# Wider score passes, joined weights and moved means in the first two units of a fused attention and MoE kernel

## The chip, the cores and the metric

The kernel runs on one core of one Trainium2 chip. A core has a matmul engine (TensorE, PE in the profile, with its weight loads as PEld), a vector engine (VectorE, DVE), an activation engine (ScalarE, ACT), a general one (GpSimd, POOL) and a queue that issues the transfers (SyncE, SP). The metric is the device time of one execution in microseconds; lower is better.

## The reference

Attention with a local window plus block summaries, then one expert layer (MoE) on its result. The weights are handed to the kernel as 8-byte floating-point words, and the kernel turns them into 4-byte ones itself.

```python
B, H, S, D = 4, 8, 768, 64          # batch elements, heads, positions, head size
k_sum = k.reshape(B, H, 24, 32, D).max(axis=3)      # 24 block maxima
v_sum = v.reshape(B, H, 24, 32, D).mean(axis=3)     # 24 block means
scores_l = q @ k.T / 8, masked to |i - j| < 16      # local window
scores_s = q @ k_sum.T / 8 + log(32)
a = softmax(concat(scores_l, scores_s))
x = (a @ concat(v, v_sum))           # 3072 tokens x 512
h = x @ w_in                         # 512 x 2048
out = (h - tanh(h)) @ w_out          # 2048 x 512
```

## The kernel before, in words

The work is cut into eight units of 384 rows, two to a batch element, so units 0 and 1 are the first element. A unit's attention goes over four pairs of heads (two pairs make a group), and a pair over three tiles of 128 rows. Per tile: one score product for both heads; `softmax`, whose step "min" adds the mask and takes the smallest (negated) score, then "exp", "sum guard", "inverse" and "normal"; `transpose_probs` ("p turn" on TensorE, "p out" back to SBUF); `values`. A row of scores has SC = 182 columns, but each half of a tile (64 rows) needs only N2 = 118 of them, shifted by 64 between the halves: `softmax` therefore runs "min" once for each half, and everything after on 118 columns.

The MoE of a unit goes over 16 slices f of the hidden dimension: `moe_in`, `moe_act`, `moe_split`, `moe_out`. In unit 0 the weights are used whole, in plain float32; each weight is then split into a high and a low part (`split_whole`) for the later units, which use three faster products instead of one. `convert` makes a float32 weight from the 8-byte words: "w scale" scales the high words, "w shift" shifts the result by three bits, "w low" joins the three bits from the low words, and "w sign" joins the sign. These three run on VectorE, one behind the other, for each of 32 weights.

Block means: for the first element `first_means` loads all values of a group and sums them with six products ("sum"). For the other three elements `sum_chunks` loads chunks and adds them on VectorE ("chunk sum"), and `finish_v` turns the sums with TensorE. `put_mean` writes the means into the values buffer `vw` by a transfer. `rawq` (queries) and `vw` (values) are one buffer each, used by the two groups in turn.

The order is made by a planner. The loop at the end of `program` adds tasks with their costs and dependences; `Plan.schedule` simulates the engines with these costs and a priority (the length of the way to the end, moved by the tables `BIAS` and `KB`), picks an engine where a task has several (`either`, tempered by `SL`), and the instructions are issued in the order found. Each engine then runs its own list in order. While TensorE has nothing to do in the first 100 us of that plan, "keep warm" products are put in. The MoE of unit 0 is added 22 slots behind its attention, so it runs beside the attention of unit 1. Tiles of one tag share a ring of buffers: a new tile waits until the oldest is released. All instructions of the program have one line in the profile, L64, that of a helper; tiles tell them apart: `prob` and `stat` are the softmax, `pS`, `pY`, `pT`, `pX`, `pH` banks of PSUM, `raw` the loaded weight words, `tmp` and `qa` their work buffers, `wf` whole weights, `wh` high parts, `chunk` and `vacc` the chunk sums, `xh` with `blk` the first sums.

The program is followed by a second version of itself under a condition that these inputs do not meet.

Of the kernel before, what the change touches and what calls it, by code (L numbers as in the profile page):

```python
# [12 lines left out]
U32 = mybir.dt.uint32  # L13
I32 = mybir.dt.int32
# [19 lines left out]
BIAS = {('top turn', 6): -62, ('p out', 19): -34, ('series', 46): -24, ('sum guard', 39): 21, ('p turn', 21): 39, ('q turn', 8): 13, ('square', 3): 43, ('w load', 29): 33, ('exp', 139): 10, ('x high', 7): 25, ('square', 16): -7, ('exp', 47): 33, ('series', 95): -20, ('square', 15): 11, ('w load', 17): 10, ('w sign 2', 2): 20, ('values', 23): -12, ('w scale', 7): 30, ('top turn', 4): 19, ('w load', 25): -40, ('square', 13): 19, ('inverse', 21): 44, ('p turn', 19): -20, ('w sign', 2): 26, ('out', 13): -36, ('min', 142): 21, ('series', 11): 10, ('normal', 25): -15, ('p out', 23): 32, ('pick', 8): 55, ('normal', 47): -11, ('v load', 13): 43, ('mean out', 3): 7, ('direct', 11): -29, ('w load', 15): -31, ('v load', 44): 24, ('out', 14): -34, ('exp', 44): -17, ('square', 8): 4, ('w load', 27): 16, ('min', 39): 60, ('g', 9): -24, ('inverse', 19): 36, ('direct', 14): 20, ('w high part', 23): -4, ('q high', 8): 12, ('w high part', 21): -20, ('cube', 1): 21, ('normal', 44): -4, ('in', 8): 8, ('w sign', 10): -32, ('in', 1): 24, ('normal', 24): -17, ('sum', 1): -20, ('x low', 7): -31, ('k load', 35): -9, ('square', 11): 1, ('tanh', 6): 20, ('v load', 39): -20, ('square', 9): 8, ('normal', 46): -8, ('direct', 6): 1, ('k high', 25): -5, ('q low', 6): 60, ('q high', 2): 30, ('inverse', 67): -5, ('w shift', 29): -5, ('v load', 52): 30, ('min', 5): -5, ('p turn', 8): -60, ('top put', 12): 60, ('min', 74): -30, ('chunk load', 5): -5, ('values', 17): 5, ('exp', 102): -60, ('values', 26): -30, ('square', 33): 30, ('w high part 2', 9): 5, ('inverse', 45): 15, ('normal', 83): -15, ('top put', 3): 30, ('k again', 9): 60, ('w low part 2', 0): -5, ('square', 73): -60, ('q again', 39): -60, ('values', 15): 5, ('k turn', 13): -5, ('sum guard', 15): -15, ('q again', 6): -60, ('exp', 24): -15, ('in', 28): -60, ('scores', 70): -15, ('w low part 2', 24): -60, ('scores', 43): 5, ('exp', 11): 5, ('normal', 36): -30, ('w shift', 19): 30, ('series', 24): 60, ('k high', 3): 15, ('q load', 15): -5, ('p out', 74): -15, ('out', 6): -30, ('min', 56): 30, ('w low part 2', 15): -5, ('out', 80): -30, ('scores', 23): -60, ('out', 41): -60, ('p turn', 87): 5, ('sum guard', 29): -30, ('chunk load', 23): -30, ('out', 3): 60, ('min', 60): -15, ('series', 20): 60, ('values', 9): 15, ('w high part 2', 16): -30, ('sum guard', 52): 30, ('normal', 8): -60, ('min', 33): 5, ('q again', 29): 60, ('exp', 18): 15, ('g low', 2): -30, ('q turn', 0): -15, ('k turn', 12): -30, ('values', 1): -60, ('series', 0): 30, ('k again', 6): -15, ('const', 2): 15, ('out', 295): 15, ('out', 85): 60, ('out', 2): -5, ('out', 45): 60, ('scores', 16): -30, ('v load', 51): -5, ('const', 10): -15, ('series', 99): -30, ('k high', 22): -15, ('min', 34): 15, ('w high part 2', 21): 30, ('k high', 55): -15, ('q load', 7): -5, ('inverse', 13): -5, ('k high', 27): -15, ('top put', 23): -60, ('w low', 21): 5, ('p out', 38): -60, ('out', 76): -30, ('out', 307): 15, ('x low', 2): -30, ('in', 126): -30, ('q load', 9): -30, ('out', 75): -5, ('w low', 13): -60, ('p out', 26): 30, ('exp', 75): 15, ('sum guard', 50): 60, ('w shift', 11): 5, ('values', 6): 30, ('chunk sum', 3): -30, ('inverse', 3): 30, ('sum guard', 42): -15, ('tanh', 1): 60, ('top max', 11): -15, ('w shift', 14): 15, ('v load', 27): 15, ('v load', 79): -5, ('series', 19): -15, ('sum guard', 90): 15, ('in', 66): -60, ('q again', 23): 30, ('p out', 18): 5, ('in', 35): -5, ('pad', 0): 5, ('w scale', 19): -5, ('g', 19): -5, ('in', 40): 30, ('p out', 25): -30, ('k high', 12): -30, ('v load', 60): -30, ('k load', 12): -60, ('sum guard', 74): -60, ('scores', 17): 30, ('k high', 7): -15, ('sum guard', 21): 60, ('p turn', 27): 30, ('q low', 42): 30, ('out', 87): 15, ('w high part 2', 22): 60, ('top put', 38): -15, ('w low', 2): 30, ('w high part 2', 26): -5, ('top put', 69): 15, ('top put', 39): -30, ('w scale', 2): -30, ('tanh', 15): -35, ('w high part 2', 17): -30, ('v load', 3): 15, ('p turn', 81): 15, ('min', 164): 5, ('p out', 6): 5, ('exp', 48): -60, ('exp', 176): -60, ('tanh', 77): -15, ('q again', 14): 30, ('exp', 22): -30, ('p out', 12): -30, ('exp', 43): -5, ('min', 2): 5, ('k turn', 15): 30, ('sum guard', 16): 60, ('v load', 37): 15, ('square', 23): -5, ('top put', 13): -5, ('tanh', 31): -60, ('v load', 81): 15, ('tanh', 37): -30, ('x low', 6): -30, ('tanh', 57): 15, ('w low part 2', 14): 30, ('p turn', 93): -15}  # L34
# [3 lines left out]
SL = {('sum guard', 0, 'gpsimd'): 0.6, ('top put', 1, 'vector'): 0.6, ('cube', 2, 'vector'): -0.3, ('g low', 2, 'vector'): 0.3, ('q high', 1, 'vector'): 0, ('x high', 1, 'vector'): -0.3, ('w scale', 0, 'vector'): 0.6, ('cube', 1, 'vector'): -0.3, ('big', 1, 'scalar'): -0.3, ('w low part 2', 1, 'vector'): 0.6, ('q again', 1, 'scalar'): 0.6, ('q again', 2, 'scalar'): 0, ('top put', 2, 'vector'): 0, ('w high part 2', 1, 'vector'): -0.3, ('sum guard', 1, 'gpsimd'): -0.6, ('top low', 1, 'gpsimd'): -0.3, ('k again', 1, 'gpsimd'): -0.6, ('sum guard', 2, 'gpsimd'): 0, ('q high', 0, 'vector'): 4, ('x whole', 2, 'vector'): 1.5, ('normal', 2, 'scalar'): 0, ('x high', 2, 'vector'): -0.6, ('w scale', 1, 'vector'): 2.5, ('top put', 0, 'scalar'): 0.6, ('k high', 2, 'vector'): 0.6, ('p out', 2, 'vector'): 1, ('p out', 1, 'vector'): 2.5, ('w high part 2', 2, 'vector'): 0, ('top put', 0, 'vector'): 2.5, ('k again', 1, 'scalar'): 1.5, ('k high', 1, 'vector'): 1, ('top high', 1, 'scalar'): -0.6, ('top high', 2, 'scalar'): 0.3, ('g', 1, 'vector'): 0.6, ('p out', 0, 'vector'): 1.5, ('q again', 2, 'gpsimd'): 0, ('x high', 0, 'vector'): 0.3, ('q high', 2, 'vector'): 0.3}  # L38
# [17 lines left out]
class Engine:  # L56


    def __init__(self, tc, engine):
        self._tc, self._engine = tc, engine  # L60

    def __getattr__(self, name):
        op = getattr(self._engine, name)
        return lambda *args, **kwargs: self._tc.keep_in_program_order(op(*args, **kwargs))  # L64


class Task:
    __slots__ = ("index", "costs", "go", "after", "order", "level", "count", "ready", "next", "start", "engine", "cost", "place", "out", "banks", "behind", "moves", "kind", "name")

HELD = {"w shift", "w low", "w sign", "w low part", "w low part 2", "w low part 3", "w high part", "w high part 2", "w scale", "normal", "g high", "g low", "g", "cube", "big", "k again", "q again", "top pre", "sum guard"}
# [23 lines left out]

class Plan:

    SEEN = {PE: 0.2, ACT: 0.16, DVE: 0.13, POOL: 0.1, SP: 0.95}
    ISSUE = 0.5
    QUEUE = 3.0
    AHEAD = 1.1

    def __init__(self):  # L110
# [47 lines left out]
    def schedule(self, idle):  # L158
# [49 lines left out]
        while total:  # L208
            best = None
            for e in engines:  # L210
                if able[e]:
                    now = max(free[e], min(ready(t, e) for t in able[e]))
                    if e == SP:
                        now = max(now, dma - self.QUEUE)
# [864 lines left out]
```

## Time and profile before

| | us |
|---|---|
| median of 3 runs | 762.74 |
| lowest, highest | 762.58, 763.68 |
| the profiled execution | 762.32 |
| its span, first to last instruction | 760.6 |
| TensorE busy | 718.8 (95%) |
| VectorE busy | 497.6 (65%) |
| ScalarE busy | 481.0 (63%) |
| GpSimd busy | 202.2 (27%) |

Busy times are sums over one execution. The digits of a slice are tenths of its length. Rows of a group give the tile written and those read, shapes, the count, busy time in us and mean duration in ns, and then the idle time of the engine just before, with what ended it. Rows of a timeline give start and length in us.

### The profile page before, as it was taken

The page shows a single profiled execution, that of the slowest core. Times are in us where ns is not written, and L with a number is a line of the kernel's source. Part 1 is how long each engine was busy: PE and PEld are TensorE (multiplying, and loading weights), DVE is VectorE, ACT ScalarE, POOL GpSimd, SP SyncE. Part 2 cuts the span into 40 slices and gives each one's busy share as a digit, 9 for nine tenths or more (in the row PEclk, how much of TensorE's full clock was granted, in tenths as well). Part 3 has the DMA queues.
Part 4 walks back from the last instruction along what each step waited for, and adds up shares of the span by engine and source line. Part 5 has one row for each costly group of instructions (what it writes and reads, how often), then busy time and mean ns, then how long its engine had stood idle before and what let it go on. Part 6 is the DMA issues. An engine that isn't in the chain of part 4 may idle for free. (4 is left out here: it accounts for less than half of the span.)

```text
span 760.6 us, 13191 instructions
## 1 busy us (share of the span) xinstructions
PE 718.8 (95%) x4187; PEld 584.8 (77%) x4187; DVE 497.6 (65%) x1789; ACT 481.0 (63%) x1439; POOL 202.2 (27%) x263
## 2 busy tenths in 40 slices
PE   7788889989999999999999999999999999999995
PEld 4465445456888887879888888889888888889884
DVE  1899999998853668677674658767764376751110
ACT  3667776746774676767565685768665676745442
POOL 3000000113443323332223333324223233222221
PEclk9979999999999999999999999999999999999998
DMA  8746656461110231313020131403020120101001
GB/s 218 194 115 195 197 174 210 133 144 49 43 33 1 59 84 60 83 43 99 5 60 1 39 104 30 93 17 86 1 61 1 39 63 1 39 1 42 1 0 47
DMA packets 110023, 54.56 MB, mean 72 GB/s; under 512 B 91000, under 2 KB 102520, under 8 KB 109944
## 3 DMA queue, kind: packets, MB, share of 16 engines
q1 hardware_dynamic: 109944, 53.62, 25.9%
q8 instruction: 35, 0.57, 0.3%
q14 instruction: 44, 0.36, 0.1%
HBM read 44.95 MB, written 6.29 MB: 67 GB/s over the span
## 5 line engine op out<-in xcount | busy, mean ns | idle before, releaser
L64 PE MATMUL pH<-xh,wf 128*128 128x384 f32 x548 | 186.1, 373 | 1.4 <-ACT gt L64 1.2
L64 POOL TENSOR_TENSOR gv<-gu,gt 128x384 f32<-128x384 f32 x112 | 114.2, 1020 | 243.0 <-ACT gu L64 96.1
L64 PE MATMUL pY<-wf,gh 128*128 128x512 f32 x432 | 177.4, 439 | 0.0
L64 PE MATMUL pH<-xh,wh 128*128 128x384 f32 x448 | 154.9, 346 | 0.0
L64 PE MATMUL pH<-xl,wh 128*128 128x384 f32 x448 | 151.2, 338 | 0.0
L64 PE MATMUL pY<-wh,gh 128*128 128x512 f32 x336 | 141.4, 421 | 0.0
L64 ACT ACTIVATE prob<-prob,stat 128x118 f32<-128x118 f32 x233 | 90.8, 393 | 70.7 <-DVE stat L64 64.6
L64 DVE CUSTOM_DVE_ANT_0 prob<-pS,mask 64x118 f32<-64x118 f32 x352 | 97.9, 278 | 53.5 <-PE pT L64 36.9
L64 PE MATMUL pY<-wh,gl 128*128 128x512 f32 x336 | 132.1, 393 | 0.0
L64 ACT ACTIVATE gu<-pH 128x384 f32<-128x384 f32 x128 | 62.6, 489 | 98.1 <-PE pH L64 85.0
L64 PEld LDWEIGHTS pH<-xh,wf 128*128 128x128 f32 x548 | 102.3, 189 | 20.8 <-ACT gt L64 4.7
L64 PEld LDWEIGHTS pY<-wf,gh 128*128 128x128 f32 x432 | 80.5, 189 | 21.7 <-issue 12.4
L64 DVE TENSOR_TENSOR gl<-gv,gh 128x384 fp32r<-128x384 f32 x59 | 34.3, 581 | 92.4 <-ACT gh L64 89.8
L64 PEld LDWEIGHTS pH<-xh,wh 128*128 128x128 f32 x448 | 84.3, 188 | 2.5 <-ACT prob L64 0.2
L64 PEld LDWEIGHTS pH<-xl,wh 128*128 128x128 f32 x448 | 84.1, 188 | 0.0
L64 POOL TENSOR_TENSOR gl<-gv,gh 128x384 fp32r<-128x384 f32 x53 | 54.7, 1033 | 107.8 <-ACT gh L64 89.7
L64 ACT ACTIVATE gh<-gv 128x384 fp32r<-128x384 f32 x112 | 58.2, 521 | 39.7 <-PE pY L64 38.6
L64 PEld LDWEIGHTS pY<-wh,gl 128*128 128x128 f32 x336 | 63.1, 188 | 15.3
L64 PEld LDWEIGHTS pY<-wh,gh 128*128 128x128 f32 x336 | 63.3, 188 | 9.4
L64 ACT ACTIVATE gu<-gu 128x384 f32<-128x384 f32 x128 | 66.9, 524 | 0.0
L64 ACT ACTIVATE gt<-pH 128x384 f32<-128x384 f32 x128 | 61.7, 483 | 0.0
L64 PE MATMUL pS<-k,q 128*128 128x364 f32 (+1 forms) x176 | 46.2, 343 | 10.2 <-DVE stat L64 7.3
(123 smaller groups left out, 996.7 us busy)
## 6 DMA issues: line engine op xcount, KB each, us to landing
raw<-in_moe_w_in_dram SPq DMA_DIRECT2D x16, 512.0 KB
raw<-in_moe_w_out_dram SPq DMA_DIRECT2D x16, 512.0 KB
rawq<-in_q_dram SPq DMA_DIRECT2D x48, 128.0 KB
out_dram<-tmp SPq DMA_DIRECT2D x24, 256.0 KB
chunk<-in_v_dram SPq DMA_DIRECT2D x24, 192.0 KB
raw<-in_k_dram SPq DMA_DIRECT2D x24, 192.0 KB
vw<-in_v_dram SPq DMA_DIRECT2D x40, 96.0 KB
vw<-in_v_dram SPq DMA_DIRECT2D x48, 64.0 KB
```

The lines of the kernel that those rows point to most:

```text
L64: return lambda *args, **kwargs: self._tc.keep_in_program_order(op(*args, **kwargs))
```

## The change

Units 0 and 1 make one "min" of all 128 rows and 182 columns, with a wide mask that also shuts out the columns of the other half; "exp" and "normal" run on 182 columns, in a ring of three buffers `probw`; "p turn" makes four transposes for two, and "p out" picks the right parts. A weight's low words are shifted in place, its sign is written into them as a 16-bit half, and one operation joins them with the scaled word. The means of the second element come from `first_means` as those of the first do, and both now add pairs of rows first and use three products for six. `put_mean` in units 0 and 1 copies with VectorE or ScalarE instead of a transfer. The second group of these units has its own buffers for queries and values. Fifteen late high parts of weights move into the buffers that this takes, when they are free. The last output tile goes through the buffer `qa`. The planner gets new costs, a limit of eight transfers in flight, and new tables `BIAS`, `SL` and `KB`, so the order changes in all units.

```diff
+WIDE = 2
-BIAS = {...}
+BIAS = {...}
...
+    def make_mask(mask, shift):
+        gpsimd.memset(mask, BIG if shift else 0.0)
...
-    do("const", POOL, 1.2, make_mask, w=[MASK])
+    buf(("maskw",), "wide", [P, SC])
+    do("const", POOL, 1.9, lambda: make_mask(at(("maskw",)), 64), w=[(("maskw",), 0)])
     do("const", POOL, 0.7, make_blk, w=[BLK])
+    do("const", POOL, 1.2, lambda: make_mask(mask, 0), w=[MASK])
...
+    homes, late = {}, 2 * NF - 15
+    for tag, bufs, n in (("vsum0", 1, 3), ("vsum1", 1, 3), ("wide", 1, 1), ("probw", 3, 1), ("rawq1", 1, 2), ("vw1", 1, 3)):
+        for m in range(bufs):
+            base = buf(("wh", tag, m), tag, [P, n, DM], F32R, bufs)
+            homes |= {late + x: (base, x) for x in range(n)}
+            late += n
...
+    def rawq_of(u, g):
+        return ("rawq", int(u < 2 and g == 1))
+
+    def vw_of(u, g):
+        return ("vw", int(u < 2 and g == 1))
...
-        def shift():
-            w = at(tmp).bitcast(U32)
-            vector.tensor_scalar(w, w, 3, None, op0=ALU.logical_shift_left)
-
         def low_bits():
-            low, _, w = words()
-            vector.scalar_tensor_tensor(w.bitcast(U32), low, 29, w.bitcast(U32), op0=ALU.logical_shift_right, op1=ALU.bitwise_or)
+            low, _, _ = words()
+            vector.tensor_scalar(low, low, 29, None, op0=ALU.logical_shift_right)
+
+        def sign():
+            x = bits().bitcast(U16).rearrange("p (n four) -> p n four", four=4)
+            vector.tensor_scalar(x[:, :, 1], x[:, :, 3], 0x8000, None, op0=ALU.bitwise_and)
...
-        def sign():
-            _, high, w = words()
-            vector.scalar_tensor_tensor(signed_to().bitcast(U32), high, 0x80000000, w.bitcast(U32), op0=ALU.bitwise_and, op1=ALU.bitwise_or)
+        def join():
+            low, _, w = words()
+            vector.scalar_tensor_tensor(at(to[0]).bitcast(U32), w.bitcast(U32), 3, low, op0=ALU.logical_shift_left, op1=ALU.bitwise_or)
...
-    def first_means(g, tag):
+    def first_means(b, g, tag):
...
+            x = at(base).rearrange("p h (t e) -> p h t e", t=3)
+            for t in range(3):
+                tensor.matmul(at(ps)[:NB, :HG * D], blk[:, t], x[:, :, t, :D], start=t == 0, stop=t == 2)
+
+        either("pair", {POOL: 1.77, DVE: 0.87}, lambda e: e.tensor_tensor(pairs()[0], *pairs(), op=ALU.add), w=[(base, 0)])
+        do("sum", PE, 1.3, go, r=[(base, 0), BLK], w=[(ps, 0)])
...
+            if u < 2:
+                either("mean copy", {DVE: 0.48, ACT: 0.68}, lambda e, to=to, x=x: copy(e, to(), x), r=[MEAN[g]], w=keys)
+            else:
+                dma("mean put", lambda to=to, x=x: sync.dma_start(to(), x), NT * NB * HG * D * 4, 1024, r=[MEAN[g]], w=keys)
...
+            if wide:
+                vector.tensor_tensor_reduce(at(pr)[:, a], o, at(("maskw",)), 1.0, 3e38, ALU.add, ALU.min, at(st)[:, a:a + 1])
+                return
...
+        if u < WIDE:
+            def turn():
+                t4 = at(t)[:N2].rearrange("p (f a r) -> p f a r", f=2, a=2)
+                for half in range(2):
+                    for a in range(2):
+                        tensor.transpose(t4[:, half, a], at(pr)[:, a, 64 * half:64 * half + N2], ident)
...
-        y, ys = ("y", u, i), buf(("ys", u, i), "tmp", [P, DM], F32, 2)
+        buf(ys, "qa", [P, DM], F32, 1) if (u, i) == (NU - 1, NT - 1) else buf(ys, "tmp", [P, DM], F32, 2)
...
-        if s0 is not None and not early and s0[0] % 2 == 1 and s0[0] + 1 < NU:
+        if B > 1 and j in (20, 28):
+            first_means(1, (j - 20) // 8, "pT")
+        if s0 is not None and not early and s0[0] % 2 == 1 and 1 < s0[0] < NU - 1:
```

More of the change, by code (lines that the diff above doesn't have):

```diff
@@ new lines @@
+HALF = {'const': (12, 12), 'k load': (8, 16), 'v load': (18, 36), 'chunk load': (8, 8), 'chunk sum': (8, 8), 'q load': (12, 15), 'w load': (9, 32), 'w scale': (8, 32), 'w shift': (8, 32), 'w low': (7, 32), 'w sign': (3, 20), 'w join': (3, 20), 'w high part': (3, 26), 'w low part': (3, 26), 'w sign 1': (4, 12), 'w sign 2': (4, 12), 'top pre': (16, 16), 'top turn': (4, 8), 'top max': (8, 16), 'top put': (14, 20), 'q turn': (6, 9), 'k turn': (6, 9), 'q high': (6, 9), 'k high': (12, 18), 'sum': (8, 8), 'sum out': (8, 8), 'scores': (17, 25), 'mean turn': (2, 4), 'mean out': (2, 4), 'mean copy': (8, 8), 'mean put': (0, 10), 'min': (32, 50), 'exp': (32, 50), 'sum guard': (15, 25), 'inverse': (15, 25), 'normal': (30, 49), 'p turn': (15, 24), 'p out': (15, 24), 'values': (14, 24), 'x high': (4, 8), 'x low': (4, 8), 'top high': (0, 4), 'top low': (0, 4), 'in': (3, 19), 'tanh': (2, 18), 'square': (3, 18), 'cube': (2, 18), 'series': (2, 18), 'g': (2, 17), 'big': (2, 17), 'direct': (2, 17), 'pick': (2, 17), 'out': (2, 45), 'w high part 2': (3, 6), 'w low part 2': (0, 6), 'g high': (0, 11), 'g low': (0, 10), 'q low': (0, 2), 'q again': (0, 2), 'k low': (0, 2), 'k again': (0, 2), 'y out': (0, 0), 'y store': (0, 0)}
@@ L68 @@
     __slots__ = ("index", "costs", "go", "after", "order", "level", "count", "ready", "next", "start", "engine", "cost", "place", "out", "banks", "behind", "moves", "kind", "name")
-HELD = {"w shift", "w low", "w sign", "w low part", "w low part 2", "w low part 3", "w high part", "w high part 2", "w scale", "normal", "g high", "g low", "g", "cube", "big", "k again", "q again", "top pre", "sum guard"}
+HELD = {"pair", "mean copy", "w join", "w shift", "w low", "w sign", "w low part", "w low part 2", "w low part 3", "w high part", "w high part 2", "w scale", "normal", "g high", "g low", "g", "cube", "big", "k again", "q again", "top pre", "sum guard"}
 class Clock:
@@ L108 @@
     AHEAD = 1.1
+    LANES = 8
     def __init__(self):
@@ L409, in program @@
     fixed(("mask",), [P, N2])
-    fixed(("blk",), [P, 6, NB])
+    fixed(("blk",), [P, 3, NB])
     fixed(("sums_seen",), [P, NU * NF])
@@ L593, in total @@
                     vector.tensor_tensor(m[:, 0], m[:, 0], m[:, 1], op=ALU.add)
-            do("chunk sum", DVE, 0.75 if c else 0.6, total, w=[(st, 0), (acc, 0)])
+            do("chunk sum", DVE, 1.15 if c else 1.0, total, w=[(st, 0), (acc, 0)])
     def finish_v(b, g):
@@ L675, in prep @@
             do("q low", DVE, 0.47, low, r=[(pq, 0), (qh, 0)], w=[(x, 1)])
-            either("q again", {DVE: 0.269, ACT: 0.413, POOL: 1.4}, lambda e, x=x, rows=rows: copy(e, at(x)[:64, :U], at(qh)[rows].bitcast(F32)), r=[(qh, 0)], w=[(x, 0)])
+            either("q again", {DVE: 0.269, ACT: 0.54, POOL: 1.4}, lambda e, x=x, rows=rows: copy(e, at(x)[:64, :U], at(qh)[rows].bitcast(F32)), r=[(qh, 0)], w=[(x, 0)])
         def line(j, a, piece):
@@ L710, in again @@
                     copy(e, x[64 * (1 - a):64 * (1 - a) + 64, a, 64:], x[64 * a:64 * a + 64, a, 64:].bitcast(F32))
-                either("k again", {DVE: 0.336, ACT: 0.5, POOL: 1.85}, again, r=[(kx[0], a), (kx[0], "sums%d" % a)], w=[(kx[0], "zero%d" % a)])
+                either("k again", {DVE: 0.44, ACT: 0.54, POOL: 1.85}, again, r=[(kx[0], a), (kx[0], "sums%d" % a)], w=[(kx[0], "zero%d" % a)])
     def summarize(b, p, pk, tag):
@@ L741, in summarize @@
             return
-        either("top high", {DVE: 0.09, ACT: 0.15}, lambda e: copy(e, at(th)[:, cs], at(top)[:, cs]), r=keys, w=[(th, p)])
+        either("top high", {DVE: 0.1, ACT: 0.15}, lambda e: copy(e, at(th)[:, cs], at(top)[:, cs]), r=keys, w=[(th, p)])
         either("top low", {DVE: 0.1, POOL: 0.25}, lambda e: e.tensor_tensor(at(tl)[:, cs], at(top)[:, cs], at(th)[:, cs].bitcast(F32), op=ALU.subtract), r=[*keys, (th, p)], w=[(tl, p)])
@@ L758, in prep_sums @@
             for j in range(len(kx)):
-                either("top put", {POOL: 0.36, DVE: 0.14, ACT: 0.153}, lambda e, j=j, a=a: put(e, j, a), r=keys[j], w=[(kx[j], "sums%d" % a)])
+                either("top put", {POOL: 0.36, DVE: 0.21, ACT: 0.266}, lambda e, j=j, a=a: put(e, j, a), r=keys[j], w=[(kx[j], "sums%d" % a)])
     def scores(u, p, i, tag):
@@ L777, in softmax @@
         s, pr, st = ("s", u, p, i), ("pr", u, p, i), ("st", u, p, i)
-        buf(pr, "prob", [P, 2, N2], F32, 2)
+        wide = u < WIDE
+        buf(pr, "probw", [P, 2, SC], F32, 3) if wide else buf(pr, "prob", [P, 2, N2], F32, 2)
         buf(st, "stat", [P, 4], F32, 3)
@@ L830, in values @@
             return
-        tiles = range(NT) if together else [i]
+        tiles, vw = range(NT) if together else [i], vw_of(u, p // PG)
         def go():
@@ L837, in go @@
                         c = P * n + 64 * half
[L838 to L839 removed]
+                        tensor.matmul(at(px)[64 * a:64 * a + 64, c:c + 64], at(vw)[:N2, n, half, 2 * (p % PG) + a, :], at(("pt", u, p, n))[:N2, a, half, :], start=True, stop=True)
+        do("values", PE, 1.35 if together else 0.55, go, r=[(("pt", u, p, n), 0) for n in tiles] + [key for n in tiles for half in range(2) for key in vw_keys(vw, n, half)], w=[(px, n) for n in tiles])
     def x_split(u, p):
```

120 lines of the change are left out of this document (69 added, 51 removed).

## The prediction

> **What bounds it now.** I read the page's busy times and slices first, then a table of busy time by stage.
>
> ```profile
> span 760.6 us, 13191 instructions
> PE 718.8 (95%) x4187; PEld 584.8 (77%) x4187; DVE 497.6 (65%) x1789; ACT 481.0 (63%) x1439; POOL 202.2 (27%) x263
> PE   7788889989999999999999999999999999999995
> DVE  1899999998853668677674658767764376751110
> PEclk9979999999999999999999999999999999999998
> ```
>
> TensorE looks like the bound, at 95%. But an average hides two regimes: VectorE is at 9 tenths in slices 3 to 9 (about 38 to 170 us), and only there is TensorE below 9. The stages, each row with its start and end, its length, and the busy times of PE, PEld, DVE, ACT and POOL:
>
> ```profile
> 0.00:17.00 17.00, 12.39 (x57) 7.82 (x58) 2.05 (x10) 5.22 (x13) 5.96 (x24) 1.00 0.92 234
> 17.00:61.00 44.00, 34.00 (x219) 23.55 (x218) 39.31 (x189) 27.80 (x94) 3.60 (x10) 0.84 0.58 158
> 61.00:100.00 39.00, 34.06 (x155) 18.59 (x155) 37.26 (x134) 30.64 (x89) 3.23 (x8) 1.00 0.56 174
> 100.00:135.00 35.00, 33.37 (x141) 17.25 (x137) 34.38 (x84) 24.02 (x58) 1.56 (x2) 1.00 0.71 211
> 135.00:175.00 40.00, 36.39 (x148) 21.08 (x147) 36.38 (x109) 23.41 (x66) 4.75 (x10) 1.00 0.46 124
> 175.00:200.00 25.00, 24.24 (x142) 18.76 (x141) 20.97 (x73) 18.79 (x59) 9.37 (x12) 1.00 0.16 48
> 200.00:740.00 540.00, 532.20 (x3283) 467.64 (x3282) 325.14 (x1193) 345.54 (x1048) 171.66 (x197) 1.00 0.16 41
> ```
>
> From 17 to 61 us the first unit's attention runs alone: VectorE 39.3 of 44 us, and TensorE's granted clock 0.84. From 61 to 175 us the first expert layer (MoE) runs beside the second unit's attention, with VectorE busy 108.0 of 114 us. TensorE idles 4.9 + 1.6 + 3.6 + 0.8 = 10.9 us between 61 and 200, and 7.8 us in the whole 540 after that. So the change can earn in two places: before 61, where TensorE has slack, and between 61 and 200, where at most 10.9 us are to be had and every matmul added must be paid from them.
>
> TensorE's waits up to 65 us, and what it does meanwhile (the row is of 0 to 61 us):
>
> ```profile
> PE pY L64 <- DVE stat L64: 2.8, 5, 1.3
> L64 PE MATMUL pX<-ident 128*128 128x128 f32 x58 | 12.6, 375 | 3.2 <-POOL ident L64 3.2
> ```
>
> It waits for VectorE's statistics, and 58 keep-warm matmuls (12.6 us, no result) fill gaps. Work added before 61 us can take their place.
>
> **The change, part by part.** *One pass over the score columns.* Today one head of one tile costs two half-tile minimum operations and two accumulator reads:
>
> ```profile
> 50.04 0.27 DVE L64 CUSTOM_DVE_ANT_0 prob<-pS,mask 64x118 f32<-64x118 f32 x1
> 50.25 0.07 DVE L64 DVE_READ_ACCUMULATOR2_ANT stat<- 64x1 f32 x1
> 50.34 0.28 DVE L64 CUSTOM_DVE_ANT_0 prob<-pS,mask 64x118 f32<-64x118 f32 x1
> 50.66 0.69 DVE L64 SCALAR_TENSOR_TENSOR qa<-raw,qa 128x512 uint32<-128x512 uint32 x1
> L64 DVE DVE_READ_ACCUMULATOR2_ANT stat<- 64x1 f32 x52 | 4.0, 77 | 0.0
> ```
>
> From 50.04 to 50.66 is 0.62. One pass over 182 columns pays one fixed part and 64 more columns. VectorE's price of a column comes from two rows of plain operations, below (553 ns for 384 columns, 691 for 512): 1.08 ns, so 0.07. That is 0.30 + 0.07 = 0.37, and 0.25 is saved. There are 52 / 2 = 26 such heads before 61 us (last row above, of 0 to 61 us), 48 in the two units: 6.5 and 12.0 us of VectorE.
>
> The price is that exponentials and normalisations run over 182 columns too (at the same column price 0.07 each, on ACT 48 x 0.07 = 3.4 us; on VectorE half of that, as its in-place scalar operations run at twice the rate, 1.7 us), and that each tile needs four transposes for two. TensorE's rows, the first two of 61 to 175 us:
>
> ```profile
> L64 PE MATMUL pT<-ident,prob 128*118 128x128 f32 x26 | 5.1, 278 | 3.8 <-DVE prob L64 3.0 <-DVE top L64 0.8
> L64 PE MATMUL pT<-vacc,ident 96*24 96x64 f32 x16 | 1.3, 221 | 0.0
> L64 PE MATMUL pY<-xh,blk 128*24 128x256 f32 x12 | 2.8, 380 | 0.0
> ```
>
> A transpose costs 5.1 / 26 = 0.20, so 24 more in each unit are 4.8 us. In the first unit they displace keep-warm matmuls and cost nothing as long as VectorE sets the pace; if that cover is gone, 4.8 or more at the low clock. In the second unit they lie on the path: +4.8.
>
> *Weights joined in one operation.* The rows (21 of 32 weights go through tmp, 11 through qa alike):
>
> ```profile
> L64 DVE TENSOR_SCALAR tmp<-tmp 128x512 uint32<-128x512 uint32 x21 | 8.8, 423 | 0.1
> L64 DVE SCALAR_TENSOR_TENSOR tmp<-raw,tmp 128x512 uint32<-128x512 uint32 x21 | 14.3, 683 | 0.1
> L64 DVE SCALAR_TENSOR_TENSOR wf<-raw,tmp 128x512 uint32<-128x512 uint32 x21 | 14.4, 688 | 0.1
> L64 DVE TENSOR_SCALAR tmp<-raw 128x512 f32<-128x512 f32 x2 | 0.8, 421 | 0.0
> L64 DVE TENSOR_REDUCE vacc<-chunk 96x64 f32<-96x512 f32 x24 | 25.1, 1058 | 1.4 <-PE pT L64 1.2
> L64 DVE TENSOR_TENSOR vacc<-vacc 96x64 f32<-96x64 f32 x18 | 5.0, 278 | 0.6
> ```
>
> Today 0.42 + 0.68 + 0.69 = 1.79 a weight. After: two one-source operations that write every second word (the sign step one 16-bit half of it), then a join like today's last step, 0.69. No row writes with such gaps. Two rows bound it. Reading every second word costs nothing (421 ns beside 423 for adjacent words); reading 64 words apart, as the chunk sum does, takes 1.06 for the same 512 elements. Nearest is the first, a step of two words, so 0.42 each: 1.53 a weight, 0.26 saved, 8.3 us over 32 (27 of them after 61 us: 7.0). At the other end 2.81 a weight, +32.6 us; nothing makes it cheaper than 0.42 at this rate. The join no longer waits for a chain through tmp, and raw buffers stay held about as long.
>
> [...]
>
> *Second element's means on TensorE.* Eight chunk sums (1.04 each before 175 us) and six adds of 0.22 to 0.28 leave VectorE, about 9.7 us: half (4.5) before 61 us. Instead come four pair additions over 768 columns. Rows for those and for the copies:
>
> ```profile
> L64 DVE TENSOR_TENSOR gh<-gu,gt 128x384 f32<-128x384 f32 x16 | 8.9, 553 | 2.2 <-PE pY L64 2.1
> L64 DVE TENSOR_TENSOR wf<-wf,wh 128x512 fp32r<-128x512 f32 x31 | 21.4, 691 | 0.2
> L64 POOL TENSOR_TENSOR gv<-gu,gt 128x384 f32<-128x384 f32 x112 | 114.2, 1020 | 243.0 <-ACT gu L64 96.1
> L64 ACT ACTIVATE wh<-wf 128x512 fp32r<-128x512 f32 x30 | 18.8, 629 | 10.9 <-DVE wf L64 10.8
> ```
>
> 0.97 each on VectorE, or at most 2.04 on POOL, which is idle there; the first element's two fall into the start, where VectorE is idle. On TensorE the first element's two sums halve (-1.4 each); the second's add 2.8 and drop 1.3: +1.5 after 61 us. Eight mean copies replace eight DMAs: on VectorE 0.42 + 0.13 = 0.55 each, on ACT about 0.9; taken half and half, 2.2 us of VectorE, 1.5 of them before 61. SP's queue loses those eight issues and the eight chunk loads, and gains two.
>
> *Own buffers for the second group.* Queries and values no longer wait for the first group's last use. This shows in no single wait; nothing saved is counted, nothing lost either: the loads move into stretches where DMA is at 0.56 to 0.71. The late high parts of weights now wait for these buffers; they are needed one unit later.
>
> *Start and end.* Two stretches of the timeline:
>
> ```profile
> 13.30 2.77 PE L64 MATMUL pY<-xh,blk 128*24 128x256 f32 x12
> 13.82 1.17 ACT L64 ACTIVATE k<-pH 64x384 f32<-64x384 f32 x4 [0.94 <-DVE th L64]
> 16.00 0.88 PE L64 MATMUL pY<-k,q 128*128 128x364 f32 x2
> 750.72 3.53 SPq L64 DMA_DIRECT2D out_dram<-tmp  x3
> 751.76 0.40 PE L64 MATMUL pY<-wh,gl 128*128 128x512 f32 x1
> 753.29 0.60 ACT L64 ACTIVATE tmp<-pY 128x512 f32<-128x512 f32 x1 [1.90 <-PEq L292]
> ```
>
> The first scores stand behind the second sum; keys are ready at 14.99, so 0 to 1.0 can go: -0.5. POOL builds the wide mask ahead of the old one, some 12 more operations; with 6.0 of the first 17 us busy it is done before the first minimum operation. At the end TensorE is done at 752.16, but the third output tile waits until 753.29 for a tmp buffer still being stored. With a buffer of its own it starts 1.1 earlier: -1.1 (bounds 0 and -1.1).
>
> *The sum.* Before 61 us VectorE loses 6.5 + 4.5 + 1.3 (five weights) and gains 0.8 + 1.5: net -10.0 of 39.3. Not all becomes time, since ACT (27.8 busy) gains about 3 and would itself fill over 90% of 34 us; I take 70%, -7.0 (bounds -10 and -2). Between 61 and 200, VectorE loses 7.0 + 5.5 + 5.2 and gains about 2, falling from 108 to some 92 of 114; TensorE gains 4.8 + 1.5 = 6.3 of work. If two thirds of its 10.9 us idle go, the stage yields 7.2 - 6.3: -0.9 (bounds -4.6 and +6.3). After 200 the order is drawn anew over 7.8 us of idle: 0 (bounds -2.5, +2.5). Together -0.5 - 7.0 - 0.9 + 0 - 1.1 = -9.5. The profiled execution took 762.3 (span 760.6 and 1.7 around it), 0.4 below the median shown, 762.7: 762.3 - 9.5 gives **752.8 us**.
>
> **Rivals.** *More of the idle goes:* every term near its good bound, -1 - 10 - 4.6 - 1.1 = -16.7, 745.6, down to 743 with a better later order. For it: VectorE's cover of both stages. Against: ACT and the transposes fill up behind it.
>
> *The relief is eaten:* TensorE's 6.3 us stand in full because its idle stays. Either the idle is mere latency (-0.5 - 7.0 + 6.3 - 1.1, 760.0), or the gapped writes run at one element a cycle, 0.69 as in the two-source rows: 2.07 a weight, which cancels the relief after 61 and a quarter of that before it, 762.0.
>
> *Slower by the gapped writes:* at 1.06 each, as the 64-word reads, the weights cost VectorE 32.6 more against 15 to 16 saved by all else: some +17 on an engine that is 95% busy, about 778. It decides from 0.80 us an operation on, where 0.50 a weight eats those 16 us. Against it stands the 421 ns row.
>
> **How the numbers follow.** Forecast (747 to 759) 0.64; more idle gone (743 to 747) 0.10; relief eaten (759 to 763) 0.16, about half within 0.2% of before, which is all that a measurement can tell from no change; slower 0.10. Faster 0.83, same 0.07, slower 0.10. The range 745 to 761 leaves out half of the second case, a quarter of the third and all of the fourth, 0.19.
>
> **What would show it.** A minimum operation of 128x182 at about 0.34 us, 48 times; the two gapped operations at 0.42 (0.69 or above 0.8 names the rival); the first matmul into pH at 52 to 55 us rather than 60.4; VectorE near 80% between there and 165; TensorE's idle there under 5 us; the last output tile right behind its last matmul. The forecast is wrong if pH starts no earlier than 58, or if the idle after it stays.

## The result, and the profile after

The kernel after takes 739.96 us (median of 4 runs, 739.65 to 741.52) against 762.66 (4 runs, 762.11 to 763.68): ratio 0.9705, 95% interval 0.9688 to 0.9722. The forecast was 752.8 with a range of 745 to 761, so the kernel is 5 us faster than the range allowed. The profiled execution of after took 741.52 us, the slowest of its four, with a span of 740.0 for 760.6.

Busy times and slices from the page of after:

```profile
span 740.0 us, 13051 instructions
PE 711.1 (96%) x4205; PEld 589.0 (80%) x4205; DVE 508.6 (69%) x1788; ACT 461.0 (62%) x1388; POOL 148.0 (20%) x229
PE   7888988999999999999999999999999999999995
DVE  3789999678876689577765786677665557753332
```

VectorE's stretch of nines is slices 4 to 7 (before, 3 to 9), and TensorE reads 9 from slice 8 on (before, from slice 10). Next the stages, cut at the first product of the expert layer into `pH`; columns as in the first table of stages (start and end, length, busy times with counts of PE, PEld, DVE, ACT and POOL, granted clock, share of the DMA engines, GB/s). The first row of each pair of fences is from the timeline and gives that product. After:

```profile
49.56 5.33 PE L67 MATMUL pH<-xh,wf 128*128 128x384 f32 x16
```

```profile
0.00:49.60 49.60, 39.00 (x270) 27.96 (x271) 32.76 (x134) 28.21 (x93) 16.94 (x56) 0.93 0.89 212
49.60:180.00 130.40, 121.92 (x514) 70.52 (x512) 113.15 (x316) 87.43 (x239) 10.92 (x19) 0.99 0.52 152
200.00:730.00 530.00, 529.12 (x3295) 472.10 (x3294) 344.80 (x1279) 328.60 (x1007) 111.49 (x143) 1.00 0.17 42
```

and before:

```profile
60.40 2.74 PE L64 MATMUL pH<-xh,wf 128*128 128x384 f32 x8
```

```profile
0.00:60.40 60.40, 45.80 (x274) 31.00 (x275) 40.76 (x198) 32.42 (x106) 9.50 (x34) 0.89 0.67 179
60.40:200.00 139.60, 128.66 (x577) 76.06 (x576) 129.58 (x396) 97.47 (x274) 18.96 (x32) 1.00 0.50 146
200.00:730.00 530.00, 522.20 (x3235) 458.84 (x3234) 323.92 (x1190) 341.21 (x1037) 169.63 (x195) 1.00 0.17 42
```

The 20.6 us of span divide as follows. The first product into `pH` comes 10.8 us earlier. From there to the end of the second unit's stage (180 after, 200 before) TensorE idles 8.5 us (130.4 less 121.9) for 10.9: -2.4. After 200 the idle falls from 7.8 us (530 less 522.2) to 0.9: -6.9. TensorE's busy time from its first `pH` product on is 672.1 (711.1 less 39.0) for 673.0 (718.8 less 45.8): -0.9. From its last product to the end of the span it is 9.0 for 8.4: +0.6. That makes -20.4, the rest is rounding of the cuts. The prediction had -7.5, -7.2, 0, +6.3 and -1.1 in these places. The start was better than forecast, the idle beside the second unit went less, TensorE's busy time did not rise although products were added, and 6.9 us came from a place where nothing had been put.

### The profile page after: what moved, and what is told of

The parts are those of the page before. It is cut to its first block, busy times and chain, and to the rows that moved or that the text cites. A ratio compares the mean times of both kernels' runs of the same rounds, so it can differ in the third digit from the quotient of the medians.

```text
span 740.0 us, 13051 instructions
## 1 busy us (share of the span) xinstructions
PE 711.1 (96%) x4205; PEld 589.0 (80%) x4205; DVE 508.6 (69%) x1788; ACT 461.0 (62%) x1388; POOL 148.0 (20%) x229
## 4 chain that ended last, share of the span: by engine, by line
PE 80%; DVE 10%; DMA 3%; SPq 2%; ACT 2%; issue 1%; POOL 1%; DVEq 0%; ACTq 0%
PE pY L67 33%; PE pH L67 33%; PE pS L67 6%; PE pT L67 4%; PE pX L67 3%; DVE raw L67 3%; DVE wf L67 3%; SPq L67 2%; DMA raw<-in_moe_w_in_dram 1%; DVE probw L67 1%; DMA raw<-in_moe_w_out_dram 1%; DMA vw<-in_v_dram 1%; DVE vacc L67 1%; DVE gh L67 0%; DVE stat L67 0%
## 5 line engine op out<-in xcount | busy, mean ns | idle before, releaser
L67 PE MATMUL pH<-xh,wh 128*128 128x384 f32 x252 | 88.2, 350 | 0.0
L67 PE MATMUL pH<-xl,wh 128*128 128x384 f32 x252 | 85.0, 337 | 0.0
L67 PE MATMUL pY<-wh,gh 128*128 128x512 f32 x168 | 70.9, 422 | 0.0
L67 PE MATMUL pY<-wh,gl 128*128 128x512 f32 x168 | 66.3, 394 | 0.0
L67 DVE TENSOR_TENSOR gv<-gu,gt 128x384 f32<-128x384 f32 x68 | 38.9, 572 | 20.5 <-ACT gu L67 13.4
L67 POOL TENSOR_TENSOR gv<-gu,gt 128x384 f32<-128x384 f32 x44 | 45.3, 1029 | 34.6 <-DVE gl L67 16.1
L67 PEld LDWEIGHTS pH<-xh,wh 128*128 128x128 f32 x252 | 47.4, 188 | 2.2 <-issue 0.5
L67 PEld LDWEIGHTS pH<-xl,wh 128*128 128x128 f32 x252 | 47.3, 188 | 0.0
L67 ACT ACTIVATE probT<-pT 118x256 f32<-118x256 f32 x86 | 32.6, 379 | 20.9 <-PE pT L67 20.8
L67 PEld LDWEIGHTS pS<-k,q 128*128 128x128 f32 x176 | 30.7, 190 | 13.1 <-issue 5.1
```

## The experiments

Times are medians; ratios are against runs of before on the same chip, with 95% intervals, and a difference in us is 762.7 times what the ratio lacks to 1.

### Parts against order

Two kernels exchange the tables `BIAS`, `SL` and `KB`: one is after with the tables of before, the other before with the tables, costs and transfer limit of after. Two more have all tables empty.

```diff
 after_oldtables (after)             before_newtables (before)
-BIAS, SL, KB = <those of after>     -BIAS, SL, KB = <those of before>
+BIAS, SL, KB = <those of before>    +BIAS, SL, KB = <those of after>; costs and LANES of after
 after_notables (after), before_notables (before)
+BIAS, SL, KB = {}, {}, {}
```

> The changed kernel with the three old tables of the planner (BIAS, SL, KB); operations, buffers and costs are those of the change. Theory 'parts': the operations and buffers bring the gain, the tables little: 740 to 745 us, first MoE product near 50 us. Theory 'order': the tables bring the 7 us of idle lost after 180 us and some of the early start: 748 to 756 us, with TensorE idle after 180 us back at 5 us or more.

> The kernel before with the new tables, the new costs of the steps that both kernels have, and the limit of eight transfers; operations and buffers as before. Theory 'parts': 758 to 770 us (tables made for other tasks may even cost time). Theory 'order': 750 to 757 us, with the idle after 200 us (7.8 us before) down to 1 to 3 us.

> The changed kernel with all three tables empty. Together with the kernel before with empty tables it prices the parts without any tuned order. 'Parts': 745 to 755 us and about 20 below the other one. 'Order': 755 to 765 us, about 12 below the other one.

> The kernel before with all three tables empty. 'Parts': 765 to 775 us, about 20 above the changed kernel with empty tables. 'Order': about 12 above it.

| | us | ratio |
|---|---|---|
| after_oldtables | 746.05 | 0.9775 (0.9759 to 0.9791) |
| before_newtables | 750.22 | 0.9839 (0.9823 to 0.9856) |
| after_notables | 761.93 | 0.9986 (0.9974 to 0.9998) |
| before_notables | 775.43 | 1.0173 (1.0150 to 1.0195) |

My first reading was that the parts are worth 10 to 17 us and the order 5 to 12. That compares kernels which differ in more than the tables: after_oldtables and after_notables still had the new costs, before and before_notables the old ones. The idle after 200 us gave the hint; these are the same rows of after_oldtables and before_newtables:

```profile
200.00:730.00 530.00, 528.09 (x3284) 470.54 (x3284) 316.19 (x1155) 343.23 (x1051) 177.24 (x218) 1.00 0.17 42
```

```profile
200.00:730.00 530.00, 527.28 (x3288) 469.49 (x3287) 351.38 (x1299) 335.68 (x1034) 108.91 (x141) 1.00 0.17 42
```

1.9 and 2.7 us of idle, for 7.8 before. One has the old tables and the other the old operations, so neither explains it. Common to them are the costs and the limit.

### Single parts in the order of after

In these four the emitted instruction changes but not its planned cost, so the order is that of after.

```diff
 f_halves: the wide minimum as two operations, one for each 64 rows, all 182 columns
-vector.tensor_tensor_reduce(at(pr)[:, a], o, at(("maskw",)), ...)
+for half in range(2):
+    rows = slice(64 * half, 64 * half + 64)
+    vector.tensor_tensor_reduce(at(pr)[rows, a], o[rows], at(("maskw",))[rows], ...)
 f_turns0 (f_turns1: u == 1): each of the four transposes made twice in that unit
-for half in range(2):
+for half in (0, 1, 0, 1) if u == 0 else (0, 1):
 f_sign32: the sign joined with 32-bit words
-vector.tensor_scalar(x[:, :, 1], x[:, :, 3], 0x8000, None, op0=ALU.bitwise_and)
+vector.scalar_tensor_tensor(low, high, 0x80000000, low, op0=ALU.bitwise_and, op1=ALU.bitwise_or)
```

> The changed kernel in its own order, but each minimum operation of the first two units is made as two operations on 64 rows each, still over 182 columns: 48 more operations and 48 more accumulator reads of VectorE, about 0.30 us each by the changed kernel's back-to-back starts (0.27 to 0.30 us), 13 to 14 us of VectorE. Theory 'VectorE is still the limit of the first two units': the time rises by 8 to 14 us, to 748 to 754. Theory 'the order and TensorE limit now': by under 4 us, 740 to 744.

> The changed kernel in its own order, with the four transposes of each tile of the first unit made twice: 48 more of about 0.15 to 0.20 us, 7 to 10 us of TensorE. If they lie under VectorE and the transfers there, as the prediction had it for the first unit, the time rises by under 3 us (740 to 743); if TensorE sets the pace there, by 7 to 10 (747 to 750).

> The same with the transposes of the second unit made twice: 48 more, 7 to 10 us of TensorE. The prediction put this unit's transposes on the path: +7 to +10 (747 to 750). If VectorE's waits still cover some of them there: +2 to +6.

> The changed kernel in its own order, with the sign of a weight joined by one two-source operation on whole words for the one-source operation on 16-bit halves, which took 746 ns in the profile of the changed kernel. By the row of the other two-source operations it takes 0.69: 32 x 0.06 = 1.8 us less of VectorE. 'VectorE is still the limit': 1 to 2 us faster, 738 to 739. 'Order and TensorE limit': no change, 740.

| | us | ratio |
|---|---|---|
| f_halves | 755.1 | 0.9916 (0.9897 to 0.9934) |
| f_turns0 | 739.3 | 0.9714 (0.9694 to 0.9735) |
| f_turns1 | 740.41 | 0.9717 (0.9699 to 0.9735) |
| f_sign32 | 740.96 | 0.9730 (0.9709 to 0.9751) |

The groups of the minimum, of after and then of f_halves (0 to 200 us, engine VectorE):

```profile
L67 DVE CUSTOM_DVE_ANT_0 probw<-pS,wide 128x182 f32<-128x182 f32 x32 | 10.1, 342 | 1.6 <-PE pS L67 1.2
L67 DVE CUSTOM_DVE_ANT_0 probw<-pY,wide 128x182 f32<-128x182 f32 x16 | 5.4, 338 | 2.6 <-PE pY L67 2.1 <-DVE pY L67 0.2
```

```profile
L67 DVE CUSTOM_DVE_ANT_0 probw<-pS,wide 64x182 f32<-64x182 f32 x64 | 22.1, 345 | 2.6 <-PE pS L67 1.2
L67 DVE CUSTOM_DVE_ANT_0 probw<-pY,wide 64x182 f32<-64x182 f32 x32 | 11.0, 345 | 1.3 <-PE pY L67 0.4
```

48 operations more, 33.1 us for 15.5. With their reads VectorE is busy 529.1 us in all for 508.6, 20.5 more, and the kernel is 15 to 16 us slower than after (755.1 for 739.96; 16.1 by the ratios). In this order VectorE in the first two units is the limit, for about three quarters of what is added. Doubling the transposes of either unit moves nothing beyond the noise, where the prediction had put those of the second on the path. (The granted clock of f_turns0 was 0.994 to 0.997, that of after 0.988 to 0.993, which may have paid for part of what was added there.) The sign with 32-bit words is 684 ns for 746, about 2 us of VectorE, too little to be seen in the time.

### One part taken back, and the costs alone

```diff
 a_onebuf (after): one buffer for both groups
-return ("rawq", int(u < 2 and g == 1))   and the same for "vw"
+return ("rawq", 0)
 a_chunks (after): second element's means by chunk sums
-if B > 1 and j in (20, 28): first_means(1, (j - 20) // 8, "pT")
-if s0 is not None and not early and s0[0] % 2 == 1 and 1 < s0[0] < NU - 1:
+if s0 is not None and not early and s0[0] % 2 == 1 and s0[0] < NU - 1:
 a_oldweights (after): "w shift", "w low", "w sign" as before
 before_newcosts (before): costs of after and its limit, old tables
+LANES = 8
-now = max(now, dma - self.QUEUE)
+now = max(now, dma - self.QUEUE, landed[-self.LANES])
... (lines that keep the list of landings)
-do("min", DVE, 0.62 if edge else 0.39, ...)
+do("min", DVE, 0.6 + 0.07 * edge, ...)
-do("chunk sum", DVE, 0.75 if c else 0.6, ...)
+do("chunk sum", DVE, 1.15 if c else 1.0, ...)
 ... w scale on ACT 0.52 -> 0.57, mean out 0.28 -> 0.39, exp 0.385 -> 0.39
 ... q again ACT 0.413 -> 0.54; k again DVE 0.336 -> 0.44, ACT 0.5 -> 0.54
 ... top high 0.09 -> 0.1; top put DVE 0.14 -> 0.21, ACT 0.153 -> 0.266; normal 0.16 -> 0.19
```

> The kernel after, but the second group of units 0 and 1 shares its buffers for queries and values with the first, as before; the order is planned again with the tables of after. Theory VectorE: the buffers are worth nothing by themselves, as the prediction counted, so 740 to 744, where up to 4 us are what any new plan loses under tables that were drawn for another program. Rival loads: the transfers run denser in the first 61 us (a share of 0.84 to 0.91 for 0.58) because the second group's loads need not wait; with one buffer the share falls back to 0.7 or less, the first matmul into pH comes at 53 or later for 49.6, and the time is 745 or more.

> The kernel after, but the block means of the second element come from chunks added on VectorE, as before; the order is planned again with the tables of after. Theory VectorE: it gets back eight chunk sums and six adds, 9.7 us, less the pair additions that it did, 1 to 2, so 6 to 9 us later: 746 to 749, the first matmul into pH at 52 to 55. Rival order: the relief of VectorE has cover, and the time is 740 to 743.

> The kernel after, but each weight is made as before: shift, low bits and sign, the last two with two sources. By the traces that takes 1.79 us of VectorE a weight for 1.86 with the joined form, 2.4 us less over 32, so the joined form is worth nothing: 738 to 743, and what it is off from after is also a gauge of what a new plan moves under these tables. Rival: the joined form earns by its waits (low bits and sign need only the raw words, not the scaled word), then 744 or more.

> The program before with its own tables, but planned with the new costs (means out 0.39 for 0.28, chunk sums 1.0 to 1.15 for 0.6 to 0.75, sums 0.60 to 0.67 for 0.39 to 0.62 and so on) and with the limit of eight transfers in flight. Theory costs: the idle of TensorE after 200 us came from a plan that took some work for cheaper than it is, so it closes here too, to 3 us or less, with no new table: 754 to 758. Rival tables: the costs alone change little, the idle after 200 stays at 6 to 9, and the time is 760 to 764; the 10 to 13 us that the new order is worth then need the tables. If it comes out slower than 764, old tables and new costs do not fit each other and the two can't be parted this way.

| | us | ratio |
|---|---|---|
| a_onebuf | 741.68 | 0.9723 (0.9698 to 0.9747) |
| a_chunks | 747.82 | 0.9794 (0.9763 to 0.9824) |
| a_oldweights | 740.05 | 0.9696 (0.9670 to 0.9722) |
| before_newcosts | 747.66 | 0.9805 (0.9778 to 0.9832) |

The joined weights and the buffers are worth nothing that shows; with one buffer the DMA share between 17 and 61 us is still 0.80, and the first `pH` product comes at 50.39, so the rival of the loads falls. Taking back the means costs some 7 us under these tables, and as the two other kernels were planned anew under the same tables and lost at most 1.7, most of that is the part and not the new plan. The surprise is before_newcosts. The program before, none of its operations touched, falls by 15 us when it is planned with other numbers. The forecast of 754 to 758 for it was too careful by half.

### Which costs

```diff
 before_mincost (before)
-do("min", DVE, 0.62 if edge else 0.39, ...)
+do("min", DVE, 0.6 + 0.07 * edge, ...)
 before_limit (before): LANES = 8 and its line, nothing else
 before_jitter (before)
-do("exp", ACT, 0.385, ...)
+do("exp", ACT, 0.39, ...)
 before_costs (before): all the costs of before_newcosts, without the limit
 before_choices (before): of these only q again, k again, top high, top put, normal
 after_oldplan (after): tables and costs of before for every task both have, no limit
```

> The program before, planned with one other cost: the minimum operation of a head at 0.60 (0.67 at the edges) for 0.39 (0.62), as the trace has it; 192 heads, so the old plan left out some 35 us of VectorE's work. Theory costs: this error is most of what before_newcosts took away (15.0), so 747 to 753, with TensorE idle after 200 us at 4 or less. Rival limit: it does little, 758 to 764. Rival luck: any value may come, and before_jitter is then far from 762 as well.

> The program before, planned with the exponential at 0.39 for 0.385, a change that carries no knowledge of the chip. Theory costs: a new draw of the order alone moves little, 759 to 766, or it loses, since the tables were drawn for the old costs. Rival luck: it falls to 755 or below, and then what before_newcosts gained need not be the costs.

> The program before with the limit of eight transfers in flight in the planner, and nothing else. Theory costs: the limit bears on the loads of the first 200 us only, and gives little: 758 to 764. Rival limit: the plan had counted on loads landing earlier than the queues let them, so this is most of the 15.0: 747 to 753.

> The operations and buffers of the kernel after under the planner of before: old tables, old costs for every task that both have, no limit of transfers. Its difference to before is what the parts alone give. The sum of the prediction without its term for the order says 762.6 less 9.5, so 753, with TensorE idle after 200 us still at 6 or more. Rival: the parts give most of the result, 742 to 747, and the new costs gain little on top of them. If the parts alone give under 3 (760 or more), they need the order to become time at all.

> The program before, planned with all the new costs but without the limit of transfers. Theory costs: the limit is not needed, 746 to 751. Rival, both are needed: 753 or more, since a plan with true costs but loads that land too early puts work ahead of its data.

> The program before, planned with the new costs of the tasks that may go to more than one engine alone: the second copies of queries and keys (ScalarE 0.54 for 0.413 and 0.5, VectorE 0.44 for 0.336), the block maxima put into the keys (VectorE 0.21 for 0.14, ScalarE 0.266 for 0.153), the normalisation on VectorE (0.19 for 0.16). Theory choices: the plan gave work to the wrong engine, and these alone bring 746 to 753, with TensorE idle after 200 us at 4 or less. Rival sum: no single group does it, the plan has to be true as a whole, and this gives 755 to 763, as the minimum operation alone did.

| | us | ratio |
|---|---|---|
| before_mincost | 759.53 | 0.9959 (0.9941 to 0.9976) |
| before_jitter | 761.78 | 0.9995 (0.9982 to 1.0008) |
| before_limit | 761.07 | 0.9988 (0.9972 to 1.0004) |
| after_oldplan | 761.36 | 0.9973 (0.9954 to 0.9993) |
| before_costs | 748.20 | 0.9808 (0.9784 to 0.9832) |
| before_choices | 760.88 | 0.9972 (0.9957 to 0.9987) |

The limit is not needed. Two new draws of the order that carry little or nothing of the costs, the jitter and the limit, moved 0.4 and 0.9 us, both within the noise, so a new draw by itself is not seen to bring 15; more draws were not made. The costs together bring 14.6 us; the minimum alone 3.1 and the choices alone 2.1. And the operations of the change under the old plan bring 2.1 us, where their sum had been 9.5. The measured corners, as differences to before in us:

| | old costs, old tables | new costs, old tables | new costs, new tables |
|---|---|---|---|
| operations of before | 0 | -14.9 | -12.3 |
| operations of after | -2.1 | -17.2 | -22.5 |

("New costs" includes the limit here.) Read along the change: truer costs some -15, the operations some -2 on top, and the new tables another -5, which they give to the new operations only (for the old ones they are, if anything, a loss). Read down the columns, the operations are worth 2 us under the old plan, 2 under the new costs with the old tables, and 10 under all of the new plan: they have no price of their own.

Where the costs earn shows in the stages of before_costs, to be set against those of before:

```profile
60.05:200.00 139.95, 133.97 (x603) 81.19 (x602) 130.51 (x396) 100.47 (x284) 22.60 (x34) 1.00 0.50 148
200.00:730.00 530.00, 527.90 (x3285) 469.57 (x3284) 314.85 (x1166) 346.31 (x1053) 176.83 (x217) 1.00 0.17 42
```

Its first `pH` product comes at 60.05, so it begins no earlier than before, but TensorE then idles 6.0 for 10.9 us up to 200, and 2.1 for 7.8 up to 730: 10.6 in all. What TensorE waited for between 200 and 730 (us in total, times, longest), in before, in before_newcosts and in after_oldplan:

```profile
PE pS L64 <- DVE stat L64: 5.7, 12, 1.3
```

```profile
PE pS L64 <- DVE stat L64: 0.9, 2, 0.5
```

```profile
PE pS L67 <- DVE stat L67: 6.2, 12, 1.8
```

A score product waits for its bank `pS`, and the last reader of a bank is the minimum. The old plan held a minimum for 0.39 us of VectorE; the groups of before between 200 and 740 say what it takes:

```profile
L64 DVE CUSTOM_DVE_ANT_0 prob<-pS,mask 64x118 f32<-64x118 f32 x264 | 73.4, 278 | 50.6 <-PE pT L64 36.9 <-PE pS L64 8.0
L64 DVE DVE_READ_ACCUMULATOR2_ANT stat<- 64x1 f32 x264 | 20.4, 77 | 0.0
```

Two operations and two reads a head are 0.71 us by their own durations, 0.62 from start to start. So the plan thought a bank free before it was, and TensorE stood in front of it, 12 times and 5.7 us in all (first of the three rows above). With this one cost mended (before_mincost) the idle is more than halved:

```profile
200.00:730.00 530.00, 526.46 (x3274) 466.00 (x3273) 324.30 (x1185) 348.18 (x1062) 177.75 (x213) 1.00 0.17 43
```

3.5 for 7.8, but the kernel gains only 3.1 us. In the profiled run (760.99 us, 1.5 above the median) TensorE's idle from its first `pH` product to 200 us rose by 1.0, and the granted clock there reads 0.96 for 1.00, an estimated 5 us of TensorE's 127 busy (127 x 0.04):

```profile
61.10:200.00 138.90, 126.95 (x546) 74.07 (x544) 126.25 (x377) 92.72 (x260) 15.42 (x28) 0.96 0.51 147
```

The operations of after under the old plan have the idle undiminished:

```profile
0.00:56.55 56.55, 43.09 (x283) 29.89 (x284) 31.24 (x138) 33.15 (x106) 19.44 (x52) 0.94 0.90 214
56.55:200.00 143.45, 132.45 (x588) 78.68 (x587) 123.06 (x353) 94.18 (x266) 19.09 (x30) 0.99 0.46 130
200.00:730.00 530.00, 522.08 (x3235) 461.46 (x3234) 322.75 (x1188) 340.59 (x1039) 171.96 (x199) 1.00 0.17 42
```

11.0 and 7.9 us. VectorE has 154.3 us of work in the first 200 for 170.3: 16 us less, as the prediction had worked out for everything but the weights (15 to 16). TensorE starts the expert layer only 3.9 us earlier and has 5.4 us more to do from there on (721.5 - 43.1 for 718.8 - 45.8).

The costs change the granted clock too. The keep-warm products of the first 100 us, in before and in before_costs:

```profile
L64 PE MATMUL pX<-ident 128*128 128x128 f32 x58 | 12.6, 375 | 3.2 <-POOL ident L64 3.2
```

```profile
L64 PE MATMUL pX<-ident 128*128 128x128 f32 x106 | 16.6, 299 | 3.8 <-POOL ident L64 3.2 <-ACT xh L64 0.6
```

A plan that sees VectorE's true load sees TensorE idle earlier and puts in more of them, 106 for 58, and each is shorter. The granted clock of the whole run is 0.993 to 0.995 in all five runs of before_costs, and 0.983 to 0.993 in the 15 of before beside them. But the time does not come from there. The stage of before_costs ahead of its first `pH` product:

```profile
0.00:60.05 60.05, 47.79 (x321) 32.73 (x322) 39.94 (x196) 31.18 (x104) 9.83 (x37) 0.97 0.66 176
```

The clock differs here, 0.97 for 0.89 in before, and yet that product comes only 0.35 us earlier. From it to 730 us both kernels read 1.00 (rows above). In that part TensorE is busy 668.7 us (716.5 less 47.8) for 673.0, with the same products: 4.3 less. With the 10.6 of idle and the 0.35 at the start, less 0.4 at the end, that makes the 14.9 us between the spans (760.6 and 745.7). The busy time falls with the number of TensorE's waits behind the first `pH` product: 35 in before (673.0), 33 in before_jitter (672.8), 28 in before_choices (671.0), 18 in before_costs and 13 in before_newcosts (668.7 both). So, as an estimate from before and before_costs (4.3 / 17), a wait costs some 0.25 us of busy time besides its own length. It would fit that products overlap in the records: between 200 and 730 us of after one follows the last every 161 ns (529.12 / 3295), while no group of them there has a mean under 221 ns. That this is the cause was not tried.

## Why the prediction was wrong, point by point

**The term that failed** is "After 200 the order is drawn anew over 7.8 us of idle: 0 (bounds -2.5, +2.5)". The same costs are in the diff, but I took the new order as a draw without direction. It had one: truer costs, worth 14.6 us on the old operations, of which 5.7 lie after 200. With it failed the way the sum was made, which took TensorE's busy time as fixed but for the products added: +6.3 was forecast there, -0.9 came, while with fewer waits the same products kept TensorE busy for less (668.7 us with 18 waits, 673.0 with 35). These two places make 14.1 us of error, against a miss of 10.9 in all; the start adds 3.3, and the idle beside the second unit and the end give back 6.5. The evidence stood in the prediction itself, where a head of the minimum was measured at 0.62 us, while the code planned it at 0.39; the two were never set side by side. The chunk sum was the same: 1.06 in the trace, 0.60 to 0.75 in the plan.

**The relief before 61 us** (-7.0 at a conversion of 70%) rested on a saving of VectorE that was right in size, the weights apart, and wrong in what it does by itself. With the old plan the start moved by 3.9 us, with the new costs and old tables to 58.12, by 2.3, and with all of the new plan by 10.8, of which the new plan gives the old operations 4.5 (before_newtables, 55.86). A shorter operation does not make an earlier product unless the order lets the product move up. The rival "the relief is eaten", its idle mere latency, gave 760.0, close to what the operations alone measured, 761.4, with the idle unchanged as it says; but the start had moved by half of what it took.

**Transposes of the second unit, +4.8 on the path, and means, +1.5.** As products they are there, but smaller. These rows of after are from its first `pH` product on:

```profile
L67 PE MATMUL pT<-ident,probw 128*118 128x128 f32 x48 | 7.4, 277 | 0.8 <-DVE probw L67 0.6 <-DVE top L67 0.2
L67 PE MATMUL pT<-vsum,blk 128*24 128x256 f32 x12 | 3.0, 382 | 0.0
```

A transpose took 0.154, not 0.20, so 48 are 2.6 us more than the 24 of before, and the sums take 3.0 for 1.3: together 4.3 for the 6.3 forecast. They do not lie on the path in the order of after: f_turns1 adds as many transposes again and gains or loses nothing. Nor does TensorE's busy time show them, as the new plan has 13 waits behind the first `pH` product for 35, which at the estimated 0.25 us takes off 5.5. Under the old plan, with 28 waits, the busy time rises by 5.4, at a granted clock of 0.99 up to 200 us.

**The minimum** was right: 0.34 us, 48 of them (rows above). So was half a column's price for the normalisation on VectorE: two in a row took 0.51 to 0.58 us at 182 columns, most of them 0.53 or 0.54, for 0.46 or 0.47 at 118 in before, some 0.55 ns a column ((0.54 - 0.47) / 128) for the 1.08 of the two-source rows. **The weights** were half right. After, 0 to 180 us:

```profile
L67 DVE TENSOR_SCALAR raw<-raw 128x512 uint16<-128x512 uint16 x32 | 23.2, 746 | 0.1
L67 DVE SCALAR_TENSOR_TENSOR wf<-tmp,raw 128x512 uint32<-128x512 uint32 x21 | 14.4, 692 | 0.1
L67 DVE TENSOR_SCALAR raw<-raw 128x512 uint32<-128x512 uint32 x32 | 13.5, 426 | 3.4 <-DMA raw<-in_moe_w_out_dram 2.8 <-DMA raw<-in_moe_w_in_dram 0.6
L67 DVE COPY vw<-mean 24x768 f32<-24x768 f32 x7 | 4.7, 677 | 0.1
```

The low bits, writing every second word, take 0.43 as forecast, and the join 0.69. The sign, writing one 16-bit half in four, takes 0.75 and not 0.42, so a weight costs 1.86 for 1.79: a loss of 2.2 us over 32 where 8.3 had been saved in the sum. The price that "names the rival", 0.69, is that of the two-source rows; what it is in cycles no run shows. It was reached by one of the two operations, yet it did no harm, and a_oldweights is as fast as after. The mean copies were 0.68 and not 0.55.

At a step of two words, 426 ns is the price of adjacent words in before (423), and in f_sign32 an operation with both sources and its result in every second word took 684, for 683 of the join beside it.

**Second element's means:** 9.7 us less for VectorE, half of it before 61, was right in kind: with the chunk sums back (a_chunks) VectorE is busy 521.1 us for 508.6, and 7 us are lost.

**Own buffers:** nothing was counted, and nothing shows: a_onebuf, 741.68. **The end:** the last tile follows its last product at once, as forecast (two rows of the timeline of after, TensorE's last product and ScalarE's copy):

```profile
730.62 0.40 PE L67 MATMUL pY<-vw,gl 128*128 128x512 f32 x1
...
731.05 0.60 ACT L67 ACTIVATE qa<-pY 128x512 f32<-128x512 f32 x1 [0.40 <-PE pY L67]
```

but the span ends 9.0 us after TensorE, for 8.4 before, so the 1.1 did not become time in this profile. **Signs named in advance:** the first `pH` product came earlier than 52 (49.56); VectorE was busy 87% from there to 180 us (113.2 of 130.4), not near 80; TensorE's idle beside the second unit stayed at 8.5, where under 5 had been forecast, so by the prediction's own second sign it was wrong here too; the idle after 200 went.

**What stays open:** which of the other costs carry the remaining 9 us or more of the 14.6 (chunk sum, scaling of weights, mean out, and any two together were not run; the exponential alone is before_jitter), and why TensorE's busy time for the same products is less where it waits less often. None of these runs is faster than after beyond the noise (f_turns0 739.3, a_oldweights 740.05).

## What to carry to other kernels

Where a planner makes the order, set its cost of each frequent operation beside the row of the trace before anything else; here planning the old operations with truer costs was worth seven times what the new operations gave alone. What an operation made shorter is worth depends on the plan that it stands in (here 2 us under the old one, 10 under the new), so a part is priced with its order, and a comparison that changes both tells nothing of either until the other corners are run.

## What the runs showed of the hardware that I had not expected

A minimum over 64 rows takes as long as one over 128 (345 and 342 ns for 182 columns). A one-source operation on every second 32-bit word, in place, runs as fast as on adjacent ones (426 and 423 ns for 512), while the same count of 16-bit halves, one in four, takes 746, longer than a two-source operation with 32-bit words that does the same work (684). A mean copied on 24 rows of 768 columns takes 677 ns on VectorE. A plan that put in more keep-warm products, 106 for 58, had them at 299 ns each for 375, at a granted clock of 0.97 for 0.89 ahead of the first `pH` product, and that product came no more than 0.35 us earlier. And from that product on the same products kept TensorE busy 668.7 us with 18 waits among them and 673.0 with 35.
